# The first pair of token blocks taken block by block over four weight groups, with three attention tiles moved among its products

## The chip, the cores and the metric

The kernel runs on one core of a Trainium2 chip. The metric is device time in microseconds: 1663.98 us is the median of 3 runs (1659.61 to 1665.5). The profiled execution took 1663.56 us; the time from its first instruction to its last, the span, is 1661.8 us.

## The reference

Three layers follow one another on 4608 tokens of width 512.

```python
# 1. attention in chunks of 64 tokens, 8 heads of 64
scores = scale * np.matmul(q_c, k_c.transpose(0, 1, 2, 4, 3))
attn = softmax(scores);  out = np.matmul(attn, v_c)     # -> x, 4608 x 512
# 2. squared ReLU, 512 -> 2048 -> 512
h = np.maximum(x @ w_in, 0.0);  x = h * h @ w_out
# 3. gated unit, 512 -> 1536 -> 512
gate = 1 / (1 + np.exp(-(x @ w_gate)));  out = gate * (x @ w_val) @ w_out
```

The weights arrive as 64-bit floating point numbers and are turned into 32-bit ones on the chip.

## The kernel before

**Number format.** A 32-bit product is made of three products of a reduced format (fp32r). Each operand x is therefore split into a high part, a copy on ACT (L437), and a low part, x minus the high part on DVE (L442).

**Blocks of the product.** A matrix product is done on 2 by 2 blocks with seven products in place of eight. This needs sums of weight blocks (operands "s", "t" and "d", built from POOL's additions at L451) and differences of token blocks. The first pair of token blocks is the exception. It uses the eight plain products, with operand "a" (upper weight blocks) and "l" (lower ones), and no sums.

**A weight tile.** `to_float32` loads 512 KB of a 64-bit weight and turns it into 32 bits: two ACT instructions (L484, L488), three on DVE (L491, L493, L500), one addition on POOL (L507). `split` then makes the high part on ACT and the low part on DVE. So an operand costs DVE four instructions. A group of `w_in` has two such tiles; there are G1 = 8 groups.

**Attention.** A tile has 128 tokens and six tiles are one pair of blocks (BL1 = 384 tokens, three tiles each). Its steps are: load k, q (SP), transpose both on PE and copy on ACT, scores on PE ("S"), a softmax of six DVE instructions (L803 to L812) with one on ACT, a transpose ("T"), load v, the product with v ("X"), and two copies into `raw1[0]` (tiles 0 to 2) or `raw1[1]` (tiles 3 to 5). `attend(0)` does tiles 0 to 5 ahead of all products, `attend(1)` tiles 6 to 11 among the first pair's products, and so on.

**The first pair.** For every group g, `plain_unit` does four results: upper and lower weight block by token block 0, then the same by token block 1. Each result is two calls of `multiply`, six matmuls of 384 columns each.

**What sets the order.** All work is described as jobs, and a planner (`Plan.run`) writes the order out once, before anything runs on the chip. Matmul jobs of the products form one stream that is kept in order; attention's matmuls come in where their written due time ("nominal") is smallest among what is ready. Every other job gets its due time from the job that needs it. An engine takes the ready job that is due first. A job that allocates memory may run only when it is due within its `look` (loads without one: LOOK, others: NEAR). A job that is due further ahead than FAR must leave FLOOR = 8 KB per partition free. `late` in `weight_group` is the look of the sums and of s, t and d. All loads and stores are issued by SP, in the order written.

**After the first pair** come pairs 1 to 5 with seven products (to about 500 us), `w_out` of layer 2 (`long_units`, to about 860 us; its operands are built again from DRAM by `w1out`), the two products of the gate (to about 1390 us), and the last product (`wo`, loaded by `brought`).

Of the kernel before, what the change touches and what calls it, by code (L numbers as in the profile page):

```python
# [51 lines left out]
class Plan:  # L52
# [252 lines left out]
        self.order = order  # L305
        return order

    LOOK, NEAR, HOLD, FAR, FLOOR = 60.0, 15.0, 8.0, 40.0, 8 * 1024

    def stuck(self, t, free, ready, heads, streams, shift):  # L310
        live = {}
# [21 lines left out]
def tile_attention_relu2_glu(  # L333
# [13 lines left out]
    B, H, S, D = q.shape  # L347
# [10 lines left out]
    BL1 = 384  # L358
    TILES = BL1 // P
    scale = 1.0 / float(D) ** 0.5  # L360

    w1i, w1o, wg, wv, w2o = (
        w.bitcast(I32) for w in (moe_w_in, moe_w_out, moe2_w_gate, moe2_w_val, moe2_w_out)
    )
    F1 = moe_w_out.shape[0] // P
    F2 = moe2_w_out.shape[0] // P
    G1, G2 = F1 // 2, F2 // 2
# [530 lines left out]
                self.finish(self, 1, 0, None)  # L898


    def plain_unit(ops, xs, n, per, finish):
        u = Unit(ops, xs, n, per, finish, "")
        for row, col in ((0, 0), (1, 0), (0, 1), (1, 1)):
            ps = psum("C")
            for half in range(2):
                multiply(ps, ops["al"[row]], half, xs[f"B{half + 1}{col + 1}"], n, half == 0, per)
            finish(u, row, col, ps)
# [129 lines left out]
    with tc.manual_schedule():  # L1037

        per1, per, per_h = 0.1735, 0.227, 0.1195
# [5 lines left out]
        w1 = {}  # L1045
# [25 lines left out]
        def attend(s):  # L1071
            for i in range(2 * TILES):
                def nominal(what, i=i):
                    slot = 7 * i + WHEN[what]
                    if s == 0:
                        return -40.0 + 2.0 * i + {"k": 0, "S": 2, "T": 6, "X": 8}[what]
                    if s == 1:
                        return slot * SLOT * 8 / 7
                    return span0 + (s - 2) * span + slot * SLOT
                attention(2 * TILES * s + i, raw1[i // TILES], i // TILES, nominal)  # L1080
# [4 lines left out]
        def finish0(g):  # L1085
            def finish(u, row, col, ps):
                n, f = BL1, g + row * G1
                t = sbuf(n, "e")
                copy(u.words(t), [t], u.words(ps), [ps], n, func=ACTF.Relu)
                if row == col:  # L1090
                    binary("DVE", u.words(t), u.words(ps), u.words(t), ALU.mult, n, [t], [t, ps])
                else:
                    copy(u.words(t), [t], u.words(t), [t], n, func=ACTF.Square, soon=4.0)
                a = col * BL1
                d = gb[f, col] = Buf(name="g")
                dma(lambda: gd[f][:, a:a + n], lambda: at(t), [t], [d], size=P * n * 4, soon=6.0)
            return finish

        attend(0)
        first_xs = {}  # L1100
        for (r, c), x in blocks1(raw1).items():
            name = f"B{r + 1}{c + 1}"
            first_xs[name] = slots1["T1" if name == "B12" else name]
            for op, (src, off) in zip(first_xs[name], x):
                split(op, src, BL1, off=off)
        for g in range(G1):
            w1[g] = weight_group(w1i, g, G1, f"wi{g}", True, look=30.0, late=60.0)
            if g == 1:
                attend(1)
            plain_unit(w1[g], first_xs, BL1, per1, finish0(g))  # L1110
        state = {}

        def unit1(s, g):
# [23 lines left out]
        def brought(back, look):  # L1137
            got = [{} for _ in back]
            for kind in "astd":
                for ops, b in zip(got, back):  # L1140
                    ops[kind] = b[kind](look=look)
            return got


        raws1 = [sbuf(2 * BLK, "wr")], [sbuf(BLK, "wf")], [sbuf(2 * BLK, "ws") for _ in range(2)]
        w1f = [float32_in_dram(rows(w1o, f), f"wf{f}", 130.0, raws1) for f in range(F1)]
# [22 lines left out]
        def y_of(m, a, n):  # L1169
            return [yb[m, b] for b in range(a // BL1, (a + n - 1) // BL1 + 1)]  # L1170

        w1out = [weight_group(None, f, G1, f"wo{f}", True, look=55.0, raws=raws1, by=rows, have=w1f) for f in range(G1)]
        long_units([
            (lambda s=s: Long(w1out, blocks_g(s), BL1, per1, finish_y(s), {"P5": "DVE", "P6": "DVE"})) for s in range(pairs1)
        ])
# [73 lines left out]

        wo = brought(back_o, 80.0)

        def last_blocks(s):
            wide = len(s) == 2
# [68 lines left out]
```

## Time and profile before

| what | value |
|---|---|
| median of 3 runs | 1663.98 us |
| profiled execution | 1663.56 us |
| span of it | 1661.8 us |
| PE busy | 1621.5 us, 98% |
| DVE busy | 1375.4 us, 83% |
| ACT busy | 979.9 us, 59% |
| POOL busy | 822.3 us, 49% |

PE is the matrix engine, PEld its weight loads, DVE the vector engine, ACT the scalar engine, POOL the GpSimd engine, SP the queue that issues transfers. "PEclk" is the granted clock of PE as a share of the full 2.4 GHz; 0.5 would be a stretch wholly at 1.2 GHz. "DMA" is the mean busy share of the 16 transfer engines, as recorded; it can read a little above 1. A row of a timeline gives the start, the duration, the engine, the line, the operation, what is written and read, and in brackets how long the engine was idle before it and what ended that.

### The profile page before, as it was taken

How to read it: one execution, taken by the hardware profiler on the slowest of the kernel's cores; microseconds unless marked ns; L12 is line 12 of the kernel's file. 1: busy time of each engine (PE TensorE's matmuls, PEld its weight loads, DVE VectorE, ACT ScalarE, POOL GpSimd, SP SyncE). 2: the span in 40 equal slices, each digit the busy share in tenths (PEclk: the TensorE clock that was granted, in tenths of full speed). 3: DMA queues.
4: the chain of work that ended last, by engine and by line, in shares of the span. 5: the costliest groups of instructions: out<-in, count | busy, mean ns of one | idle time of the engine just before them, and what ended most of it. 6: DMA issues, size and time to landing. Idle time of an engine off the chain costs nothing. (4 is left out here: it accounts for less than half of the span.)

```text
span 1661.8 us, 30842 instructions
## 1 busy us (share of the span) xinstructions
PE 1621.5 (98%) x10500; PEld 1463.8 (88%) x10500; DVE 1375.4 (83%) x2002; ACT 979.9 (59%) x1968; POOL 822.3 (49%) x636
## 2 busy tenths in 40 slices
PE   7999999999999999999999999999999999999998
PEld 5999999989899999999988888888888888778887
DVE  7998677767789999999999797754777757999995
ACT  6876666665676555565566566544565544454543
POOL 1552103030454443543577677733675646867672
PEclk8999999999999999999999999999999999999999
DMA  9855557666794755855976744496256568665572
GB/s 233 236 137 154 148 149 195 174 185 183 241 303 160 231 191 176 265 184 192 314 264 215 235 169 153 169 342 245 103 202 219 208 244 324 177 183 131 168 176 48
DMA packets 390798, 333.36 MB, mean 201 GB/s; under 512 B 234736, under 2 KB 325616, under 8 KB 390640
## 3 DMA queue, kind: packets, MB, share of 16 engines
q1 hardware_dynamic: 390640, 331.38, 64.4%
q8 instruction: 83, 1.36, 0.3%
q14 instruction: 75, 0.61, 0.1%
HBM read 209.13 MB, written 122.16 MB: 199 GB/s over the span
## 5 line engine op out<-in xcount | busy, mean ns | idle before, releaser
L507 POOL TENSOR_TENSOR wf__3381<-wf__3381,wr__3279 128x512 int32<-128x512 int32 x16 | 21.3, 1331 | 176.5 <-DVE wf__3381 L500 83.6
L507 POOL TENSOR_TENSOR wf__7084<-wf__7084,wr__6460 128x512 int32<-128x512 int32 x18 | 28.4, 1581 | 67.8 <-DMA g__7033<-gd 15.3
L507 POOL TENSOR_TENSOR wf__6751<-wf__6751,wr__6460 128x512 int32<-128x512 int32 x18 | 26.5, 1473 | 65.8 <-DVE wf__6751 L500 37.4
L451 POOL TENSOR_TENSOR raw__514<-raw__674,raw__514 128x384 f32<-128x384 f32 x20 | 23.5, 1195 | 69.2 <-DVE B__762 L442 48.8
L488 ACT ACTIVATE wr__6460<-wr__6460 128x512 int32<-128x512 uint32 x36 | 23.9, 663 | 0.0
L451 POOL TENSOR_TENSOR ws__7370<-wf__6751,wf__7084 128x256 f32<-128x256 f32 x18 | 16.6, 924 | 12.8 <-DVE wx__7053 L442 12.5
L442 DVE TENSOR_TENSOR wx__7053<-ws__7370,wx__7053 128x512 fp32r<-128x512 f32 x18 | 17.7, 984 | 4.1 <-ACT wx__7053 L437 2.2
L442 DVE TENSOR_TENSOR wx__7583<-ws__7370,wx__7583 128x512 fp32r<-128x512 f32 x18 | 18.7, 1041 | 1.9 <-ACT wx__7583 L437 1.9
L442 DVE TENSOR_TENSOR wx__7387<-wf__7084,wx__7387 128x256 fp32r<-128x256 f32 x18 | 17.3, 958 | 2.7 <-ACT wx__7387 L437 2.7
L451 POOL TENSOR_TENSOR ws__7370<-ws__7370,wf__6751 128x256 f32<-128x256 f32 x18 | 15.7, 870 | 1.3
L507 POOL TENSOR_TENSOR w__647<-w__647,wraw__374 128x512 int32<-128x512 int32 x1 | 1.5, 1469 | 29.7 <-ACT w__684 L484 29.7
L493 DVE TENSOR_SCALAR wf__7084<-wf__7084 128x512 int32<-128x512 int32 x18 | 14.2, 790 | 0.6
L484 ACT ACTIVATE wf__6751<-wr__6460 128x512 f32<-128x512 f32 x18 | 12.0, 665 | 4.7 <-POOL ws__7370 L451 4.7
L500 DVE SCALAR_TENSOR_TENSOR wf__7084<-wr__6460,wf__7084 128x512 int32<-128x512 int32 x18 | 14.4, 801 | 0.2
L500 DVE SCALAR_TENSOR_TENSOR wf__6751<-wr__6460,wf__6751 128x512 int32<-128x512 int32 x18 | 14.2, 790 | 0.1
L442 DVE TENSOR_TENSOR B__762<-raw__514,B__762 128x384 fp32r<-128x384 f32 x6 | 3.4, 566 | 13.0 <-ACT B__762 L437 13.0
L484 ACT ACTIVATE wf__7084<-wr__6460 128x512 f32<-128x512 f32 x18 | 11.9, 659 | 2.8 <-DMA wr__6460<-in_moe_w_gate_dram 2.8
L484 ACT ACTIVATE wf__3381<-wr__3279 128x512 f32<-128x512 f32 x16 | 10.6, 665 | 4.3 <-DMA wf<-wf__3381 4.2
L850 ACT ACTIVATE raw__514<-bank 128x256 f32<-128x256 f32 x36 | 12.2, 385 | 1.4 <-PE bank L835 0.5
L451 DVE TENSOR_TENSOR b__12368<-b__12368,bank 128x512 f32<-128x512 f32 x5 | 3.4, 687 | 11.3 <-PE bank L641 11.3
L493 DVE TENSOR_SCALAR wf__6751<-wf__6751 128x512 int32<-128x512 int32 x18 | 12.3, 682 | 0.6
L451 POOL TENSOR_TENSOR sums__2380<-w__1701 128x256 f32<-128x256 f32 x1 | 0.7, 737 | 23.9 <-DVE qT__2187 L751 23.9
(5780 smaller groups left out, 6526.4 us busy)
## 6 DMA issues: line engine op xcount, KB each, us to landing
ad<-wx__7053 SPq DMA_DIRECT2D x27, 512.0 KB, 5.1
ad<-wx__7583 SPq DMA_DIRECT2D x27, 512.0 KB, 4.8
wr__3279<-in_moe_w_out_dram SPq DMA_DIRECT2D x16, 512.0 KB, 4.7
wr__6460<-in_moe_w_gate_dram SPq DMA_DIRECT2D x12, 512.0 KB, 5.5
wr__6460<-in_moe_w_val_dram SPq DMA_DIRECT2D x12, 512.0 KB, 4.6
wr__6460<-in_moe_w_out_dram SPq DMA_DIRECT2D x12, 512.0 KB, 4.1
ad<-wx__7387 SPq DMA_DIRECT2D x18, 256.0 KB, 4.1
wf<-wf__3381 SPq DMA_DIRECT2D x16, 256.0 KB, 4.9
```

Of the source, the lines that this page charges most:

```text
L442: lambda: nc.vector.tensor_tensor(out=lo(), in0=at(src, n, F32, off), in1=hi().bitcast(F32), op=ALU.subtract),
L451: eng, cost(eng, n), lambda: e.tensor_tensor(out=o(), in0=a(), in1=b(), op=op),
L484: nc.scalar.activation(out=at(w), in_=t[:, :, 1].bitcast(F32), func=ACTF.Abs)
L488: nc.scalar.activation(out=low, in_=low.bitcast(U32), func=ACTF.Copy, scale=2.0**-29)
L493: nc.vector.tensor_scalar(out=wi, in0=wi, scalar1=5, scalar2=2, op0=ALU.logical_shift_left, op1=ALU.logical_shift_right,)
L500: nc.vector.scalar_tensor_tensor(out=wi, in0=words()[:, :, 1], scalar=-0x40000000, in1=wi, op0=ALU.bitwise_and, op1=ALU.bitwise_or,)
L507: nc.gpsimd.tensor_tensor(out=wi, in0=wi, in1=words()[:, :, 0], op=ALU.add)
L850: nc.scalar.activation(out=o[:, :, a:a + CH], in_=i, func=ACTF.Copy)
```

## The change

- `plain_unit` takes one token block (`col`) at a time. The order of the products becomes: groups 0 to 3 by token block 0, the same four groups by token block 1, and then groups 4 to 7 as before, block 0 and block 1 of each.
- Tiles 3 to 5 of `attend(0)` get due times among the products: their k and q transposes at -8, -5 and -2 in place of -34, -32 and -30, where the first product is due at 0 and one `multiply` counts 1.04.
- `attend(1)` is described after the third unit; its due times are the same.
- `late` of the `w_in` groups goes from 60 to 30.
- LOOK, NEAR and FAR go from 60, 15, 40 to 90, 20, 55; the look of `w1out` from 55 to 65; that of `wo` from 80 to 60.

```diff
--- before.py
+++ after.py
@@ -305,7 +305,7 @@
         self.order = order
         return order
 
-    LOOK, NEAR, HOLD, FAR, FLOOR = 60.0, 15.0, 8.0, 40.0, 8 * 1024
+    LOOK, NEAR, HOLD, FAR, FLOOR = 90.0, 20.0, 8.0, 55.0, 8 * 1024
 
     def stuck(self, t, free, ready, heads, streams, shift):
         live = {}
@@ -898,9 +898,9 @@
                 self.finish(self, 1, 0, None)
 
 
-    def plain_unit(ops, xs, n, per, finish):
+    def plain_unit(ops, xs, n, per, finish, col):
         u = Unit(ops, xs, n, per, finish, "")
-        for row, col in ((0, 0), (1, 0), (0, 1), (1, 1)):
+        for row in range(2):
             ps = psum("C")
             for half in range(2):
                 multiply(ps, ops["al"[row]], half, xs[f"B{half + 1}{col + 1}"], n, half == 0, per)
@@ -1073,7 +1073,8 @@
                 def nominal(what, i=i):
                     slot = 7 * i + WHEN[what]
                     if s == 0:
-                        return -40.0 + 2.0 * i + {"k": 0, "S": 2, "T": 6, "X": 8}[what]
+                        from_ = -40.0 + 2.0 * i if i < TILES else 3.0 * (i - TILES) - 8.0
+                        return from_ + {"k": 0, "S": 2, "T": 6, "X": 8}[what]
                     if s == 1:
                         return slot * SLOT * 8 / 7
                     return span0 + (s - 2) * span + slot * SLOT
@@ -1103,11 +1104,14 @@
             first_xs[name] = slots1["T1" if name == "B12" else name]
             for op, (src, off) in zip(first_xs[name], x):
                 split(op, src, BL1, off=off)
-        for g in range(G1):
-            w1[g] = weight_group(w1i, g, G1, f"wi{g}", True, look=30.0, late=60.0)
-            if g == 1:
+        AHEAD = 4
+        early = [(g, c) for c in range(2) for g in range(AHEAD)]
+        for i, (g, c) in enumerate(early + [(g, c) for g in range(AHEAD, G1) for c in range(2)]):
+            if c == 0:
+                w1[g] = weight_group(w1i, g, G1, f"wi{g}", True, look=30.0, late=30.0)
+            if i == 3:
                 attend(1)
-            plain_unit(w1[g], first_xs, BL1, per1, finish0(g))
+            plain_unit(w1[g], first_xs, BL1, per1, finish0(g), c)
         state = {}
 
         def unit1(s, g):
@@ -1169,7 +1173,7 @@
         def y_of(m, a, n):
             return [yb[m, b] for b in range(a // BL1, (a + n - 1) // BL1 + 1)]
 
-        w1out = [weight_group(None, f, G1, f"wo{f}", True, look=55.0, raws=raws1, by=rows, have=w1f) for f in range(G1)]
+        w1out = [weight_group(None, f, G1, f"wo{f}", True, look=65.0, raws=raws1, by=rows, have=w1f) for f in range(G1)]
         long_units([
             (lambda s=s: Long(w1out, blocks_g(s), BL1, per1, finish_y(s), {"P5": "DVE", "P6": "DVE"})) for s in range(pairs1)
         ])
@@ -1249,7 +1253,7 @@
 
 
 
-        wo = brought(back_o, 80.0)
+        wo = brought(back_o, 60.0)
 
         def last_blocks(s):
             wide = len(s) == 2
```

## Rows read from the trace of the kernel before

**Rows 1.** Page, part 1: busy time and share of the span by engine

```profile
PE 1621.5 (98%) x10500; PEld 1463.8 (88%) x10500; DVE 1375.4 (83%) x2002; ACT 979.9 (59%) x1968; POOL 822.3 (49%) x636
```

**Rows 2.** Windows of 10 us: busy time by engine, granted clock, DMA

```profile
20.00:30.00 10.00, 7.05 (x180) 5.75 (x176) 9.41 (x22) 7.19 (x17) 0.00 (x0) 0.97 1.06 268
30.00:40.00 10.00, 6.08 (x84) 4.90 (x83) 9.39 (x14) 9.41 (x21) 4.05 (x3) 0.67 1.13 272
40.00:50.00 10.00, 10.00 (x78) 9.43 (x77) 9.86 (x19) 7.75 (x17) 1.61 (x1) 0.84 1.06 267
```

**Rows 3.** Windows, cut at the end of tile 5's softmax, then to 200 us

```profile
0.00:29.15 29.15, 21.10 (x388) 16.97 (x388) 17.70 (x36) 16.73 (x31) 0.70 (x6) 1.00 1.05 215
29.15:60.00 30.85, 26.77 (x273) 24.27 (x274) 29.42 (x49) 26.80 (x57) 12.00 (x10) 0.83 1.10 278
60.00:120.00 60.00, 60.00 (x601) 57.30 (x600) 54.95 (x85) 48.14 (x101) 33.54 (x33) 1.00 0.57 155
120.00:160.00 40.00, 38.89 (x361) 36.49 (x360) 37.09 (x67) 25.42 (x56) 11.49 (x10) 1.00 0.59 157
160.00:200.00 40.00, 40.00 (x422) 37.60 (x421) 25.56 (x51) 24.31 (x56) 5.10 (x6) 1.00 0.62 159
```

**Rows 4.** Timeline of SP's queue: start, duration of the issue, transfer

```profile
9.70 2.01 SPq L415 DMA_DIRECT2D k__317<-in_k_dram  x2
...
21.87 1.79 SPq L415 DMA_DIRECT2D wraw__374<-in_moe_w_in_dram  x1
```

**Rows 5.** Timeline of ACT: first instruction on the first weight

```profile
28.07 0.66 ACT L484 ACTIVATE w__647<-wraw__374 128x512 f32<-128x512 f32 x1 [1.14 <-DMA wraw__374<-in_moe_w_in_dram]
```

**Rows 6.** Timeline of PE: transposes, scores, value product, then the first products

```profile
4.20 1.09 PE L768 MATMUL bank<-ident,k__295 128*128 128x128 f32 x4 [4.20 <-DMA k__295<-in_k_dram]
...
9.29 0.66 PE L768 MATMUL bank<-ident,q__301 128*128 128x128 f32 x4
...
10.63 1.15 PE L785 MATMUL bank<-kT__361,qT__376 64*64 64x64 f32 x32 [0.25 <-ACT qT__376 L422]
...
17.47 0.69 PE L835 MATMUL bank<-aT__480,v__311 64*64 64x64 f32 x32
...
39.50 1.31 PE L641 MATMUL bank<-B__762,wia__734 128*128 128x384 f32 x3
...
44.58 0.68 PE L641 MATMUL bank<-B__762,wil__751 128*128 128x384 f32 x3
45.10 0.68 PE L641 MATMUL bank<-B__767,wil__751 128*128 128x384 f32 x3
```

**Rows 7.** Timeline of DVE: the first softmax, then a weight tile's four instructions

```profile
9.47 0.69 DVE L803 TENSOR_REDUCE mx__372<-bank 128x8 f32<-128x512 f32 x1 [9.47 <-PE bank L785]
...
30.91 0.43 DVE L491 TENSOR_SCALAR w__684<-w__684 128x512 f32<-128x512 f32 x1
31.38 1.40 DVE L493 TENSOR_SCALAR w__684<-w__684 128x512 int32<-128x512 int32 x1
32.81 0.69 DVE L500 SCALAR_TENSOR_TENSOR w__684<-wraw__378,w__684 128x512 int32<-128x512 int32 x1
...
36.20 0.69 DVE L442 TENSOR_TENSOR wil__751<-w__684,wil__751 128x512 fp32r<-128x512 f32 x1
```

**Rows 8.** Timeline of POOL: the first weight's addition

```profile
31.02 1.47 POOL L507 TENSOR_TENSOR w__647<-w__647,wraw__374 128x512 int32<-128x512 int32 x1 [29.72 <-ACT w__684 L484]
```

**Rows 9.** Line L451 alone: results, sums and differences on DVE and POOL

```profile
0.00:60.00 60.00, 1.65 (x3) 3.77 (x4) 0.91 1.07 247
60.00:160.00 100.00, 12.12 (x22) 31.85 (x32) 1.00 0.58 155
```

**Rows 10.** PE in layer 2's second product: a window, and stalls

```profile
520.00:560.00 40.00, 38.01 (x209) 36.86 (x208) 39.05 (x66) 24.66 (x53) 15.01 (x12) 0.96 0.40 124
...
523.49 0.96 PE L961 MATMUL bank<-x__6283,wos__5934 128*128 128x384 f32 x4 [1.40 <-DVE x__6283 L442]
...
856.87 2.26 PE L961 MATMUL bank<-x__9869,wod__6479 128*128 128x384 f32 x6 [3.73 <-ACT x__7925 L437]
```

## The prediction

> **What bounds the kernel now.** I read the busy times by engine first: PE is busy 98% of the span [rows 1], so nothing but PE's own lost time can be won: idle time, and time at half clock. The windows say where it is lost. Up to 60 us PE is busy 21.10 + 26.77 = 47.87 us, 12.1 us idle; from 60 to 120 us it is never idle [rows 3]. In the slices from 30 and from 40 us the granted clock is 0.67 and 0.84 [rows 2]: after work in only 7.05 and then 6.08 of 10 us PE spent part of both slices at 1.2 GHz. Read as a mix of the two levels, that is 6.6 and 3.2 us at half speed, so with the busy share of each slice some (4.0 + 3.2) / 2 = 3.6 us of matmul time is lost. The start thus loses about 16 us. The rest of the run (1661.8 - 1621.5 - 12.1 = 28 us idle, in small stalls and the tail) is not touched directly.
>
> Of the 16 us, 4.2 go before the first k has landed [rows 6], and stay. **About 12 us is the most that the start can give back**, 0.7% of the run.
>
> What does PE wait for up to 39.50 us, where the first product starts [rows 6]? SP issues the first weight at 21.87 us, behind 18 attention loads [rows 4]; it lands at 28.07 [rows 5], 6.2 us later. The transfer engines are full meanwhile (share 1.05 and 1.10 [rows 3]). But DVE is full as well: 9.41, 9.39 and 9.86 of 10 us [rows 2], and 29.42 of the 30.85 us up to 60 us [rows 3]. So two views name two limits, transfers and DVE, and the forecast hangs on which of them the new order meets.
>
> **The change, part by part.** *Tiles 3 to 5 go among the products.* Nine loads (k, q, v of three tiles) move behind the first weights on SP's queue, and the first weight's load moves from 21.87 us to where a fourth tile's k stands now, 9.70 us [rows 4]. It lands at about 16 us. Its conversion takes what it takes now, from 28.07 us to the end of the low part shortly before the same split of the second weight at 36.20 [rows 5, 7], about 7.5 us: ready at 23.5. Token block 0 now waits for tiles 0 to 2 only; I put them at 24 us (before, PE reached the first value product at 17.47 us [rows 6], with four more tiles in the way). The first product then starts at 25 to 26 us in place of 39.50, some 14 us earlier. That is not yet time won, since three tiles' matmuls are still to be done: a tile costs PE three transposes of 0.66, scores of 1.15 and 0.69 for v, in all 3.8 us [rows 6]; three tiles 11.4 us.
>
> *Four groups by block 0, then by block 1.* No matmul is added or taken away. A triple of matmuls follows the one before it by 0.52 us [rows 6], a `multiply` is two of them, 1.04 us, and four groups by one block are 32 triples, 16.7 us. What changes is which operands must be there first. Before, two weight tiles (a and l) feed eight calls, 8.3 us of PE. Now they feed four, 4.2 us, until block 1 has its turn: for the first 16.7 us of products the conversions must come twice as fast.
>
> DVE's bill: six tiles cost it 17.70 us in 36 instructions [rows 3], 2.95 each. From 29.15 to 60 us it did 49 instructions in 29.42 us: two tiles (12 instructions, 5.9 us), three results (1.65 us [rows 9]) and eight token splits of the same 384 columns (4.4); the other 26 instructions, 17.5 us, are 6.5 weight tiles, 2.7 us each. One seen alone is 0.43 + 1.40 + 0.69 + 0.69 = 3.2 [rows 7]; the 1.40 stands beside POOL's addition of 1.47 [rows 8], and with 0.43 in its place the tile would cost 2.2.
>
> Now compare equal PE work. By 60 us PE had done tiles 0 to 6, part of tile 7, and products from 39.50 us on, some 28 triples (20.5 us less two tiles' share, over 0.52). About the same work in the new order is tiles 0 to 6 and all 32 triples of block 0 by four groups. DVE's needs for it: 7 x 2.95 + 4.4 + 4 x 0.55 + 8 x 2.7 = 48.9 us, against 17.70 + 29.42 = 47.1 before: 1.8 us more. Against that stands DVE's idle time, 60 - 47.1 = 12.9 us, of which 9.47 go before the first scores [rows 7] and stay; the earlier weights can fill the other 3.4. So the start lies between 1.8 us lost (nothing filled) and 1.6 won; if conversions met POOL less often (2.2 us each), 8 x 0.5 = 4 more are won. I take 1.5 won, by the DVE rows, which are the nearest. The bounds of this term are 12 won (PE alone limits) and 5 lost (nothing filled, and PE, in short waits, at half clock as long as now).
>
> Here a wait is added: the products are one stream in order, so when group 2's conversion is late, group 0's block 1, ready, stands behind it; only attention's matmuls can pass. From the end of block 0 PE has 16.7 us of products that need no conversion, so DVE catches up.
>
> *late 60 to 30.* The sums on POOL and s, t and d come up to 30 us later. That is 8 x (0.69 + 0.69 + 0.4) = 14 us of DVE (the 0.69 is a 512-column split [rows 7], d has half) and part of POOL's 31.85 us at L451 [rows 9]. They cost nothing where DVE has room: 2.9 us from 120 to 160 and 14.4 us from 160 to 200 [rows 3]. If that cover fails, pair 1 waits for them. I take zero, bounds 1 won (PE's 1.1 us idle from 120 to 160 [rows 3]) and 7 lost (rival C).
>
> The Trainium skill, "SBUF — State Buffer", section "SBUF: two separate sides", says that VectorE and GpSimd share a port pair that one instruction holds to its end while the other fully blocks. The row of 1.40 us beside the 1.47 us addition agrees. By that rule each POOL sum that leaves the start gives DVE up to its own length back, at most the 3.77 us of four sums before 60 us [rows 9]; the start would then win 5 in place of 1.5, still less than half a per cent.
>
> *Limits.* Each load that allocates has a look of its own, so LOOK changes nothing. NEAR lets splits and copies take memory 5 us earlier, FAR lets work 40 to 55 us ahead use the last 8 KB: no price in the trace; zero, bounds 4 us either way, one stall like that of 3.73 us at 856 us [rows 10]. `w1out` may load 10 us earlier: at 523 us PE waits 1.40 us for a split on DVE, and from 520 to 560 us it is idle 2.0 us at a granted clock of 0.96 [rows 10], 3.2 us at half speed, 1.6 lost: 3.6 in all. I take half, 2 won, bounds 0 and 3.6. `wo` from 80 to 60: PE's idle time does not show that these loads are late or early; zero, bounds as for NEAR.
>
> **Sum.** 1663.56 - 1.5 - 2 = 1660 us. The profiled execution (span 1661.8 and 1.8 around it) is 0.4 below the median of 1663.98, which I let stand.
>
> **Rivals.** *B, PE alone limits the start.* For it: PE gets products 14 us earlier. Against it: DVE's 94 to 99% from 20 us on [rows 2]. By 25.5 us PE has then done three tiles and half of tile 3, about 13.5 us, and 2 us more for the cold first matmuls (1.09 against 0.66 [rows 6]): 10 idle. If it is full from there, 16 - 10 = 6 are won, and up to 12 if more of tiles 3 to 5 comes before; I take 8. With the 2 of `w1out`: 1653.5, from 1649 to 1656.
>
> *C, slower: the work put off is owed at the border of pairs 0 and 1.* Place: 125 to 145 us, in the window in which DVE is 37.09 of 40 us busy [rows 3]. If half of the 14 us of s, t and d falls there, into 2.9 us of room, PE waits 4 us. After the stall of 3.73 us the next six matmuls took 2.26 us [rows 10] against 1.04 for two triples: 2 more for the clock. With 2.5 lost at the start: 1663.6 + 8.5 = 1672. It decides once more than 2.9 us of DVE work is put off into that window.
>
> The Trainium skill, "TensorE: Matmul & The Clock Gate", section "Part 1: The HAM clock gate (the "warmup" mystery)", says that half rate is the default and only activity lifts it, which speaks against a stream of short waits; the 0.67 after a thin slice agrees, and the 5 lost above hold it.
>
> *D, the longer limits.* Memory given out earlier holds up blocks of tokens at one or two of the later borders, 3.73 and 2 us each like the stall at 856 us [rows 10]: 1670. Against it: the loads there have their own looks, unchanged but for two.
>
> **Chances.** Forecast 0.55 (own range 1655 to 1667), B 0.29, C 0.11, D 0.05. About 0.5%, 8.3 us, is what a measurement of this kernel can tell from no change. B mostly lies beyond it (0.24), the forecast's low edge adds 0.06: faster 0.30. C and most of D: slower 0.14. The rest, 0.56, is the same. The range from 1650 to 1671 leaves out half of C and the ends.
>
> **What would show it.** The first product at 25 to 26 us (forecast and B alike); DVE over 9.4 of 10 us from 20 to 60 us with PE idle between weight tiles (forecast), or PE over 9.5 of 10 from 26 us on (B); PE's idle time up to 60 us at 9 to 13 us (forecast), 7 or less (B); a wait of PE over 2 us for an s, t or T operand between 125 and 180 us (C); the stall near 523 us gone. A first product after 30 us, or a time outside 1650 to 1671, would make it wrong.

## The result, and the profile after

The changed kernel takes 1673.08 us (median of 5 runs, 1670.61 to 1675.06) against 1662.74 us for the kernel before (5 runs, 1659.61 to 1665.5). The ratio is 1.0062, interval 1.0051 to 1.0074: **slower**, 10 us and 0.6%, outside the forecast range of 1650 to 1671. The profiled execution took 1673.64 us.

The page of the kernel after, busy time by engine, answers to [rows 1]:

```profile
PE 1624.1 (97%) x10500; PEld 1463.9 (88%) x10500; DVE 1364.1 (82%) x2002; ACT 980.9 (59%) x1968; POOL 811.2 (49%) x636
```

PE's busy time grew by 2.6 us and the span by 10.1 (1671.9 - 1661.8), so 7.5 us are new idle time. The other engines worked about as long or less.

Where the time went is read best at an equal point of the work. Layer 2's second product (L961) begins after 4704 recorded matmuls in both kernels. Windows of the two kernels up to that point, and for 56.75 us behind it; the columns are the stretch, its length, then busy us and count of PE, PEld, DVE, ACT and POOL, the granted clock, DMA share and GB/s. First the kernel before:

```profile
0.00:503.25 503.25, 482.38 (x4704) 453.40 (x4705) 397.44 (x706) 340.33 (x733) 144.76 (x138) 0.99 0.72 196
503.25:560.00 56.75, 54.76 (x305) 53.61 (x305) 55.38 (x90) 34.51 (x76) 25.20 (x20) 0.97 0.52 168
```

The same two stretches of the kernel after:

```profile
0.00:509.44 509.44, 483.84 (x4704) 454.51 (x4705) 386.86 (x707) 340.39 (x735) 142.54 (x136) 0.98 0.71 195
509.44:566.19 56.75, 52.36 (x281) 49.55 (x281) 54.24 (x86) 33.86 (x71) 25.85 (x22) 0.97 0.44 147
```

By the first L961 the new kernel is 6.2 us late: 4.7 us more idle time (25.60 against 20.87) and 1.5 us more for the same matmuls, part of them at half clock. In the next 56.75 us it does 281 matmuls in place of 305; 24 at 0.174 us (a triple of 0.52) are 4.2 us. The sum, 10.4, is the loss. The other 1100 us are even.

The first 6.2 us, by stretch. Windows of the kernel after, the first three for [rows 2], the others for [rows 3 and 10] and the end of the pairs:

```profile
20.00:30.00 10.00, 7.30 (x150) 5.93 (x148) 8.16 (x13) 8.38 (x20) 2.90 (x3) 0.90 1.17 277
30.00:40.00 10.00, 8.75 (x157) 7.68 (x160) 9.83 (x22) 9.85 (x21) 1.74 (x2) 1.00 0.94 243
40.00:50.00 10.00, 8.08 (x96) 7.23 (x89) 9.79 (x18) 8.14 (x18) 3.18 (x3) 1.00 0.92 221
...
0.00:60.00 60.00, 46.70 (x665) 40.25 (x666) 46.96 (x87) 42.94 (x87) 11.19 (x14) 0.94 1.05 236
60.00:120.00 60.00, 60.00 (x596) 56.88 (x596) 45.72 (x78) 45.36 (x92) 25.21 (x24) 1.00 0.63 169
120.00:160.00 40.00, 36.31 (x337) 34.55 (x336) 30.45 (x57) 23.89 (x54) 11.50 (x12) 0.96 0.49 134
160.00:200.00 40.00, 40.00 (x425) 37.62 (x424) 29.42 (x57) 26.84 (x61) 10.87 (x13) 1.00 0.65 165
...
520.00:560.00 40.00, 35.61 (x185) 32.80 (x184) 38.79 (x62) 21.18 (x44) 17.42 (x15) 0.96 0.29 93
```

- *Start, 0 to 60 us:* 13.3 us idle (12.1 before), but less time at 1.2 GHz. Read as a mix of the two levels, a clock of 0.94 over 60 us is 7.2 us at half speed; at a busy share of 0.78, half of it is lost, 2.8 us. Before, 0.83 over the last 30.85 us [rows 3] gave 10.5 us, 4.6 lost. So the start is even within a microsecond, 16.1 us lost against 16.7; by 120 us PE has done 1261 recorded matmuls, against 1262.
- *Border of pairs 0 and 1, 120 to 160 us:* 3.7 us idle (1.1 before) at a clock of 0.96 (1.00 before), 1.4 us by the same reckoning: 4 us lost.
- *End of the pairs, 440 us to the first L961:* the rest, some 2 us, in stalls of 1.81 us and less at 450 us and a slice behind them at a clock of 0.83.

**The start.** The weight's issue on SP, its first ACT instruction, what ACT, DVE and POOL did before the first product, and that product, from the timelines of the kernel after (start, duration, engine, line, operation; in brackets idle time and what ended it). They answer to [rows 4, 5 and 6].

```profile
9.68 1.32 SPq L415 DMA_DIRECT2D wraw__317<-in_moe_w_in_dram  x1
...
16.82 0.66 ACT L484 ACTIVATE w__477<-wraw__317 128x512 f32<-128x512 f32 x1
...
21.35 1.34 POOL L507 TENSOR_TENSOR w__477<-w__477,wraw__317 128x512 int32<-128x512 int32 x1 [20.04 <-DVE w__477 L500]
...
21.57 1.40 DVE L493 TENSOR_SCALAR w__528<-w__528 128x512 int32<-128x512 int32 x1
...
24.46 0.68 ACT L850 ACTIVATE raw__491<-bank 128x256 f32<-128x256 f32 x2
...
24.62 1.36 DVE L442 TENSOR_TENSOR wia__566<-w__477,wia__566 128x512 fp32r<-128x512 f32 x1 [0.92 <-ACT wia__566 L437]
26.70 0.43 DVE L491 TENSOR_SCALAR w__577<-w__577 128x512 f32<-128x512 f32 x1 [0.71 <-ACT w__577 L484]
...
28.56 0.60 ACT L437 ACTIVATE B__629<-raw__491 128x384 fp32r<-128x384 f32 x1
...
31.65 0.69 DVE L812 TENSOR_TENSOR a__623<-a__623,mx__371 128x512 f32<-128x512 f32 x1
32.26 0.55 DVE L442 TENSOR_TENSOR B__629<-raw__491,B__629 128x384 fp32r<-128x384 f32 x1
...
34.48 0.79 PE L641 MATMUL bank<-B__629,wia__566 128*128 128x384 f32 x3
```

The weight was there as early as forecast, and its low part was done at 26.0 us. The last piece of token block 0 was copied from 24.46 us on. But ACT then did copies of tiles 3 and 4 and parts of two weight tiles, and made the high part (B__629, L437) only at 28.56 us. DVE did the third weight tile, the softmax of tile 3 and the first steps of tile 4's without a gap, and made the low part at 32.26 us. Loads do not set the first product; the orders on ACT and DVE do.

**The border.** SP's queue in the kernel after:

```profile
121.51 8.18 SPq L415 DMA_DIRECT2D ql__1826<-in_q_dram  x16
...
131.74 0.40 SPq L415 DMA_DIRECT2D gd<-e__790  x1
132.31 0.38 SPq L415 DMA_DIRECT2D k__1981<-in_k_dram  x1
```

and PE there:

```profile
130.83 1.15 PE L785 MATMUL bank<-kT__1950,qT__1781 64*64 64x64 f32 x32 [1.36 <-ACT kT__1950 L422]
...
136.63 0.66 PE L768 MATMUL bank<-ident,k__1981 128*128 128x128 f32 x4 [2.33 <-DMA k__1981<-in_k_dram]
...
138.38 1.16 PE L641 MATMUL bank<-B__629,wia__756 128*128 128x384 f32 x3
```

One q load, issued as 16 transfers, holds SP for 8.18 us. Five stores follow, and only then the k that PE stands for; behind the stall a triple takes 1.16 us in place of 0.69. DVE had 9.5 us to spare in the window, so this is not the lack of DVE time that rival C named. Nor is it the q load alone. The kernel before has two such loads here, from 112.65 us (8.52 us) and from 126.81 us, and loses only 1.1 us in the window: PE waits there for no load that stands behind them. The second one, from SP's timeline of the kernel before:

```profile
126.81 8.88 SPq L415 DMA_DIRECT2D ql__1939<-in_q_dram  x16
```

**The entry of layer 2's second product.** PE in the kernel after, for the stall at 523 us of [rows 10], which is gone; the last row answers to its stall at 856.87 us, which is not:

```profile
530.12 0.97 PE L961 MATMUL bank<-x__6490,wos__6235 128*128 128x384 f32 x4 [0.40 <-DVE x__6490 L442]
...
535.51 0.44 PE L961 MATMUL bank<-x__6490,wos__6557 128*128 128x384 f32 x1 [0.73 <-DVE wos__6557 L442]
536.78 1.20 PE L961 MATMUL bank<-x__6490,wos__6557 128*128 128x384 f32 x4 [0.83 <-DVE x__6490 L442]
...
558.45 1.14 PE L961 MATMUL bank<-x__6800,wot__6860 128*128 128x384 f32 x5 [1.14 <-DVE wot__6860 L442]
...
867.58 1.52 PE L961 MATMUL bank<-x__8014,wod__6293 128*128 128x384 f32 x6 [3.63 <-DVE b__2909 L451]
```

One wait of 1.40 us became a row of small ones, each for a low part on DVE, which was busy 38.79 of 40 us. The stall at 867 us has about the size of the old one, but another releaser.

### The profile page after: what moved, and what is told of

It reads as the page before. It is cut to its first block, busy times and chain, and to the rows that moved or that the text cites. A ratio compares the mean times of both kernels' runs of the same rounds, so it can differ in the third digit from the quotient of the medians.

```text
span 1671.9 us, 30839 instructions
## 1 busy us (share of the span) xinstructions
PE 1624.1 (97%) x10500; PEld 1463.9 (88%) x10500; DVE 1364.1 (82%) x2002; ACT 980.9 (59%) x1968; POOL 811.2 (49%) x636
## 4 chain that ended last, share of the span: by engine, by line
PE 82%; DVE 8%; issue 3%; DMA 3%; ACT 2%; POOL 2%; SPq 1%; DVEq 0%; ACTq 0%; POOLq 0%
PE bank L641 48%; PE bank L961 29%; PE bank L785 2%; PE bank L835 1%; PE bank L819 1%; PE bank L768 1%; SPq L415 1%; DVE x__14566 L442 0%; DMA k__333<-in_k_dram 0%; DMA wr__6475<-in_moe_w_val_dram 0%; DMA yd<-c__7381 0%; POOL wf__6611 L507 0%; DMA k__299<-in_k_dram 0%; DMA gd<-c__2147 0%; DVE x__14547 L442 0%
## 5 line engine op out<-in xcount | busy, mean ns | idle before, releaser
L451 POOL TENSOR_TENSOR raw__491<-raw__774,raw__491 128x384 f32<-128x384 f32 x20 | 24.9, 1267 | 58.8 <-DVE B__629 L442 38.7
L491 DVE TENSOR_SCALAR wf__7093<-wf__7093 128x512 f32<-128x512 f32 x18 | 13.4, 744 | 8.4 <-ACT wf__7093 L484 8.4
L451 DVE TENSOR_TENSOR b__10757<-b__10757,bank 128x512 f32<-128x512 f32 x9 | 6.2, 684 | 14.7 <-PE bank L641 14.7
L451 POOL TENSOR_TENSOR ws__7383<-wf__6611,wf__7093 128x256 f32<-128x256 f32 x18 | 16.4, 912 | 0.1
L491 DVE TENSOR_SCALAR wf__6611<-wf__6611 128x512 f32<-128x512 f32 x18 | 12.6, 697 | 4.7 <-ACT wf__6611 L484 4.7
L451 POOL TENSOR_TENSOR ws__7383<-ws__7383,wf__6611 128x256 f32<-128x256 f32 x18 | 15.0, 835 | 1.1
L484 ACT ACTIVATE wf__7093<-wr__6475 128x512 f32<-128x512 f32 x18 | 11.9, 660 | 4.6 <-DMA wr__6475<-in_moe_w_val_dram 4.0
L451 DVE TENSOR_TENSOR b__11976<-b__11976,bank 128x512 f32<-128x512 f32 x5 | 3.4, 688 | 13.2 <-PE bank L641 9.5
L500 DVE SCALAR_TENSOR_TENSOR wf__6611<-wr__6475,wf__6611 128x512 int32<-128x512 int32 x18 | 13.3, 739 | 0.2
L451 POOL TENSOR_TENSOR g__7004<-g__6141,g__7004 128x384 f32<-128x384 f32 x2 | 6.2, 3118 | 14.7 <-PE bank L961 11.0
L484 ACT ACTIVATE wf__3407<-wr__3301 128x512 f32<-128x512 f32 x16 | 10.7, 666 | 4.4 <-DMA wf<-wf__3407 4.4
```

Source lines behind the costliest of these rows:

```text
L451: eng, cost(eng, n), lambda: e.tensor_tensor(out=o(), in0=a(), in1=b(), op=op),
L484: nc.scalar.activation(out=at(w), in_=t[:, :, 1].bitcast(F32), func=ACTF.Abs)
L491: nc.vector.tensor_scalar_max(at(w), at(w), TINY)
L500: nc.vector.scalar_tensor_tensor(out=wi, in0=words()[:, :, 1], scalar=-0x40000000, in1=wi, op0=ALU.bitwise_and, op1=ALU.bitwise_or,)
```

## The experiments

The first theory after the comparison was that work put off by the shorter `late` is owed at the border and at the entry; its rivals were that the new start or the limits do the harm, and, from the first experiments on, that any edit gives another order whose stalls fall anew, as if drawn by lot ("a draw" below).

"Idle" is PE's idle time, the length less PE's busy time in a window, in us. Ratios are to the kernel before, timed beside each.

| kernel | median us | ratio, interval | idle 0-60 | 120-160 | 500-560 |
|---|---|---|---|---|---|
| before | 1662.7 | 1 | 12.1 | 1.1 | 2.0 |
| after | 1673.1 | 1.0062, 1.0051 to 1.0074 | 13.3 | 3.7 | 5.6 |
| 1 before + new start + late 30 | 1689.3 | 1.0161, 1.0144 to 1.0178 | 16.0 | 5.7 | 8.6 |
| 2 before + limits | 1658.0 | 0.9972, 0.9962 to 0.9982 | 10.2 | 1.5 | 3.3 |
| 3 before + late 30 | 1671.6 | 1.0055, 1.0041 to 1.0069 | 13.2 | 5.6 | 6.8 |
| 4 before + w1out 65 | 1656.4 | 0.9964, 0.9951 to 0.9977 | 12.7 | 1.1 | 2.1 |
| 5 after, late 60 | 1670.1 | 1.0046, 1.0033 to 1.0059 | 13.0 | 1.6 | 7.8 |
| 6 after, old start, late 60 | 1662.8 | 1.0007, 0.9996 to 1.0017 | 10.6 | 1.7 | 3.2 |
| 7 before + block order | 1665.5 | 1.0020, 1.0009 to 1.0030 | 11.9 | 1.9 | 3.7 |
| 8 before, late 58 | 1662.5 | 1.0001, 0.9992 to 1.0009 | 12.5 | 1.5 | 2.9 |
| 9 before, late 45 | 1674.5 | 1.0068, 1.0053 to 1.0084 | 11.7 | 2.1 | 7.5 |
| 10 before + tiles' due times | 1677.8 | 1.0091, 1.0078 to 1.0104 | 15.3 | 4.1 | 3.2 |
| 11 after, late 32 | 1668.8 | 1.0040, 1.0028 to 1.0052 | 13.4 | 2.5 | 5.5 |
| 12 before, late 90 | 1671.1 | 1.0050, 1.0037 to 1.0062 | 13.8 | 1.7 | 10.9 |
| 13 before, margin 1.6 | 1735.7 | 1.0426, 1.0409 to 1.0442 | | | |
| 14 after, margin 1.6 | 1814.4 | 1.0903, 1.0887 to 1.0919 | | | |
| 15 before, issue 0.46 | 1664.8 | 1.0005, 0.9996 to 1.0015 | 12.2 | 1.5 | 2.1 |
| 16 after, issue 0.46 | 1662.9 | 0.9999, 0.9989 to 1.0009 | 14.1 | 1.6 | 2.9 |
| 17 before, debt 0.44 | 1666.9 | 1.0031, 1.0021 to 1.0040 | 12.4 | 1.6 | 5.9 |
| 18 after, debt 0.44 | 1677.6 | 1.0105, 1.0084 to 1.0125 | 12.2 | 4.6 | 3.7 |

The three stretches are not the whole run. From 160 to 440 us experiments 1 and 18 have 13.6 and 10.1 us idle, the kernel before 4.8, and the others but 13 and 14 1.4 to 6.2. The idle times are each of one execution, and the table leaves out time at 1.2 GHz.

**1. The start and the shorter `late`, without limits and looks.** The kernel before with the new `plain_unit`, loop and tile times, and

```diff
-            w1[g] = weight_group(w1i, g, G1, f"wi{g}", True, look=30.0, late=60.0)
+                w1[g] = weight_group(w1i, g, G1, f"wi{g}", True, look=30.0, late=30.0)
```

> The kernel before with the new start alone: products by token block over four groups, tiles 3 to 5 among them, late at 30; LOOK, NEAR, FAR and the looks of w1out and wo as before. Theory of places (each loss belongs to the edit that touches its place): the stalls of PE near 130 to 140 us stay (about 3.8 us of idle time and slow clock), the loss between 440 and 560 us (about 6 us) is gone: about 1666.5 us, 4 over before. Rival, the theory of rewriting (any edit rewrites the whole order, and stalls fall anew by chance all over the run): the first 120 us as in the changed kernel, and from there a loss or gain of up to 6 us anywhere, not tied to these two places.

1689.3 us, the slowest of the parts: 16.0 us idle at the start, 5.7 at the border, 13.6 from 160 to 440 us, 8.6 from 500 to 560. The first product stands at 37.64 us, not at 34.48.

**2. The limits alone.**

```diff
-    LOOK, NEAR, HOLD, FAR, FLOOR = 60.0, 15.0, 8.0, 40.0, 8 * 1024
+    LOOK, NEAR, HOLD, FAR, FLOOR = 90.0, 20.0, 8.0, 55.0, 8 * 1024
```

> The kernel before with LOOK, NEAR and FAR at 90, 20 and 55, and nothing else. Theory of places: the start and the border of pairs 0 and 1 as before; part of the loss at 440 to 560 us, where operands for w_out are loaded more than 40 us ahead and FAR applies: 3 us slower, about 1666. Theory of rewriting: anywhere from 1658 to 1670, with stalls at other borders than in the changed kernel.

4 us faster. The first product of this kernel, from PE's timeline:

```profile
34.47 0.67 PE L641 MATMUL bank<-B__741,wia__734 128*128 128x384 f32 x1
```

The first product comes at 34.47 us with the *old* order of tiles: the 5 us that the change seemed to win there are had by the limits alone, and PE's idle time up to 60 us is 10.2. Taken over the run, the limits by themselves cost nothing, against rival D, though 2.4 us of new idle time stand between 60 and 120 us.

**3. `late` alone.** The edit of experiment 1's diff, on the kernel before.

> The kernel before with late at 30 in place of 60, and nothing else: the sums and s, t, d of w_in come later. If the work put off is what stalls the border of pairs 0 and 1 (rival C of the prediction): 3 to 4 us of new PE idle time between 125 and 145 us, 1666 us. If the border stalls for its k loads, which this edit does not touch: no new idle time there, 1663 us give or take 2. Theory of rewriting: 1658 to 1670.

9.6 us slower, by itself as much as the whole change. PE's timeline at the border, and then the window:

```profile
136.03 0.73 PE L819 MATMUL bank<-ident,a__1980 128*128 128x128 f32 x4 [3.05 <-DVE a__1980 L812]
```

```profile
120.00:160.00 40.00, 34.37 (x326) 32.31 (x325) 35.79 (x62) 24.30 (x53) 15.99 (x16) 0.96 0.52 133
```

Here PE does wait for DVE, but for a softmax, and not for want of DVE time. DVE was busy 35.79 us in the window, less than the 37.09 before [rows 3], and stood idle before it took up this softmax, until PE had its scores:

```profile
130.41 0.69 DVE L803 TENSOR_REDUCE mx__1971<-bank 128x8 f32<-128x512 f32 x1 [0.72 <-PE bank L785]
```

The place is the same as in the kernel after, the releaser is not. That the work put off causes this wait is not shown.

**4. The look of `w1out` alone.**

```diff
-        w1out = [weight_group(None, f, G1, f"wo{f}", True, look=55.0, raws=raws1, by=rows, have=w1f) for f in range(G1)]
+        w1out = [weight_group(None, f, G1, f"wo{f}", True, look=65.0, raws=raws1, by=rows, have=w1f) for f in range(G1)]
```

> The kernel before with the look of w1out at 65 in place of 55, and nothing else. The order up to about 430 us is the same by construction, so its PE idle time up to there must be as before. By the prediction: 2 us won near 523 us, 1661. Theory of places now: the loss at 440 to 560 us comes from this edit, 4 to 6 us slower, 1667 to 1669.

6 us faster, the best kernel of all; it beats both. Its windows for [rows 10] and the 300 us behind them:

```profile
520.00:560.00 40.00, 38.87 (x220) 37.71 (x219) 39.44 (x66) 23.25 (x48) 13.52 (x12) 1.00 0.39 128
...
600.00:900.00 300.00, 297.96 (x1660) 289.77 (x1658) 290.73 (x422) 186.18 (x368) 166.99 (x124) 1.00 0.68 228
```

From 520 to 560 us it does 220 matmuls in place of 209, at a clock of 1.00, not 0.96: 11 at 0.174 are 1.9 us, the size that the forecast took. The rest is elsewhere: from 600 to 900 us PE is idle 2.0 us against 6.6, since the stall of 3.73 us at 856 us is gone. Nothing in the edit aims at that stall. Part of the gain is no matter of order: the edit leaves the order alone up to about 430 us, and the traces agree up to 120 us, where PE, DVE and SP have the same instructions in the same order. Yet in this execution the two slices of [rows 2] that had a clock of 0.67 and 0.84 read

```profile
30.00:40.00 10.00, 5.38 (x85) 4.07 (x83) 9.83 (x15) 8.94 (x20) 4.18 (x3) 0.86 1.08 268
40.00:50.00 10.00, 10.00 (x87) 9.40 (x85) 9.86 (x20) 8.51 (x19) 1.63 (x1) 0.97 1.14 277
```

By the prediction's reckoning that is 1.0 us lost to the clock in place of 3.6, so a clock term moves by some 2.5 us from one execution to the next. The 6 us of the medians stand beyond that.

**5. and 6. The kernel after with `late` 60, and that with the old start too.**

```diff
-                w1[g] = weight_group(w1i, g, G1, f"wi{g}", True, look=30.0, late=30.0)
+                w1[g] = weight_group(w1i, g, G1, f"wi{g}", True, look=30.0, late=60.0)
```

> The changed kernel with late back at 60, all else as changed. If late at 30 is what stalls the border of pairs 0 and 1 (late alone cost 9 us): the PE idle time near 125 to 150 us goes, and 5 to 9 us come back: 1664 to 1668 us, no slower than before within 0.3%. If the new start itself costs (tiles 3 to 5 and block order): 1672 or more.

> The kernel before with LOOK, NEAR, FAR, the looks of w1out and wo as changed, and the old start with late at 60. The limits alone won 4 us and w1out alone 5.6. Theory of places (gains belong to their edits and add up): 1652 to 1655. Theory of rewriting (each is one draw of an order): 1657 to 1663, no better than each alone.

With the same limits, looks and `late`, the old start takes 1662.8 us and the new one 1670.1: the new start costs 7 us. Idle time up to 60 us is 2.4 more; at 500 to 560 us, a stretch that holds no work of the start, it is 4.6 more. The border is nearly whole in both. Putting `late` back gives 3 of the 10 us back, and the intervals of experiment 5 and the kernel after overlap. The parts that gain alone (4 and 6 us) gain nothing together with the look of `wo` at 60. `wo` alone was not run; from 900 to 1400 us, experiment 6 has 7.1 us idle, experiments 2 and 4 have 6.5 and 5.3 without that edit.

**7. and 10. The start in its two halves,** first the new `plain_unit` and its loop as in the change, then the due times of tiles 3 to 5 (the edit below), each alone on the kernel before.

```diff
-                        return -40.0 + 2.0 * i + {"k": 0, "S": 2, "T": 6, "X": 8}[what]
+                        from_ = -40.0 + 2.0 * i if i < TILES else 3.0 * (i - TILES) - 8.0
+                        return from_ + {"k": 0, "S": 2, "T": 6, "X": 8}[what]
```

> The kernel before with the first pair's products by token block over four groups, tiles 3 to 5 and late as before, and no other edit. If the block order alone asks too much of DVE (twice the conversions in the first 16.7 us of products): PE idle between 40 and 60 us, 3 to 6 us lost by 60 us, 1666 to 1669 at the end. If conversions keep up because all six tiles come first: no loss by 60 us, 1662 give or take 3.

> The kernel before with the due times of tiles 3 to 5 as changed, and no other edit. Theory: moving them behind the first weights gains nothing by itself, since DVE and ACT, not the loads, set the first product; the first product comes 2 to 5 us earlier, PE lost time by 60 us the same within 1.5 us, 1662 give or take 3. If the loads had been the limit: first product at 26 us, 5 us won by 60 us, 1657.

The order by blocks costs 3.4 us, the tiles' times 15. In experiment 10 the first product comes at 40.30 us, later than before: moving tiles 3 to 5 behind the weights does not by itself bring the products forward. Neither half gains, though in the old order of results block 1, and with it tiles 3 to 5, is due four calls, 4.2 us, after the first product.

**8., 9. and 12. Other values of `late`** on the kernel before: 58, 45 and 90 in place of 60. Theory: what counts is how much work is put off, so the time grows as `late` falls. Rival: any change of the number gives another order, with stalls of its own.

```diff
-            w1[g] = weight_group(w1i, g, G1, f"wi{g}", True, look=30.0, late=60.0)
+            w1[g] = weight_group(w1i, g, G1, f"wi{g}", True, look=30.0, late=58.0)
```

> The kernel before with late at 58 in place of 60: an edit too small to move work by itself, but the planner writes a new order. Theory of places: 1662 within 1.5 us. Theory of rewriting: the time moves by 2 to 6 us either way, which would be the scatter against which every single edit's gain or loss has to be read.

> The kernel before with late at 45, half of the step. Late at 30 cost 9.6 us, late at 58 nothing. Theory of debt (work put off falls due where DVE is full, so the cost grows with the delay): 2 to 6 us slower, 1664 to 1668, with new PE idle time between 125 and 155 us. Theory of draws (each order is a new draw): no order between the steps, 1656 to 1670, and where it loses is not the border of pairs 0 and 1.

> The kernel before with late at 90, the other way. Theory of debt: the sums come as soon as their weights do, DVE and POOL have them behind them at the border of pairs 0 and 1: the 2 us lost there go or stay, 1660 to 1663. If early sums instead take DVE from the first weights: 2 to 4 us lost between 40 and 120 us, 1665.

Against 60, the values 30, 45, 58 and 90 cost 10, 12, 0 and 9 us. The longest is as bad as the shortest, so the time does not follow the work put off. But 58 moved nothing, against the rival: not every edit is a new draw of several us. The place of the loss follows it in part: at 45 and 90 the border is nearly whole (2.1 and 1.7 us idle), and the entry of layer 2 takes the loss. PE there with 90:

```profile
522.26 0.69 PE L961 MATMUL bank<-x__6481,woa__6167 128*128 128x384 f32 x1 [7.88 <-ACT woa__6167 L437]
525.94 1.97 PE L961 MATMUL bank<-x__6481,woa__6167 128*128 128x384 f32 x5 [2.99 <-DVE woa__6167 L442]
```

**11. The kernel after with `late` 32** in place of 30, the same edit.

> The changed kernel with late at 32 in place of 30, an edit too small to move work, but a new order. Theory of places: 1673 within 1.5 us, with the stalls at the border of pairs 0 and 1 and in the first unit of layer 2's second product as in the changed kernel. Theory of draws: the 10 us of the changed kernel are partly chance, 1664 to 1676, with stalls of other sizes at these two places.

4 us faster than with 30, from two units of a due time.

**13. to 18. Both kernels with a cost of the planner nudged,** in three pairs: the margin of a transfer, the cost of an issue on SP, and the share in which POOL's use of the port counts against DVE. None of these numbers changes an instruction; they change what the planner believes.

```diff
-    DMA_LATENCY, MARGIN = 2.5, 1.5
+    DMA_LATENCY, MARGIN = 2.5, 1.6
...
-        return job("SP", 0.45 * n, go, reads, writes, size=size, soon=soon, look=look)
+        return job("SP", 0.46 * n, go, reads, writes, size=size, soon=soon, look=look)
...
-                    port["debt"] += 0.45 * min(cost, max(0.0, port["DVE"] - t))
+                    port["debt"] += 0.44 * min(cost, max(0.0, port["DVE"] - t))
```

> The kernel before with the planner's margin for a transfer at 1.6 in place of 1.5: no part of the change, a new order. Theory of the change (the 10 us belong to the edits): 1662 within 2 us here, and 1673 within 2 us for the changed kernel with the same nudge. Theory of draws (each order is a draw with a scatter of several us, and before was an ordinary or a lucky one): 1658 to 1675 here, and the two kernels nudged alike differ by anything from -8 to +12.

> The changed kernel with the planner's margin for a transfer at 1.6 in place of 1.5. Theory of the change: 1673 within 2 us, 10 over its partner. Theory of draws: 1660 to 1680.

> The kernel before with the planner's cost of a transfer's issue at 0.46 in place of 0.45 us: no part of the change, a new order. Theory of the change: 1662 within 2 us. Theory of draws: 1658 to 1675, the loss mostly in the first 40 us of layer 2's second product, where the orders so far lost between 2 and 14 us.

> The changed kernel with the planner's cost of a transfer's issue at 0.46 in place of 0.45 us. Theory of the change: 1673 within 2 us, 10 over its partner, 3 to 4 us of it at the border of pairs 0 and 1. Theory of draws: 1660 to 1680.

> The kernel before with the planner's factor for time that DVE owes POOL at 0.44 in place of 0.45: no part of the change, a new order, the third such pair. Theory of the change: 1662 within 2 us. Theory of draws: 1658 to 1675.

> The changed kernel with the same factor at 0.44 in place of 0.45. Theory of the change: 1673 within 2 us, 10 over its partner. Theory of draws: 1660 to 1680, and the mean of the three differences of pairs is below 5 us.

After less before is +79, -1.9 and +10.7 us in the three pairs, a mean of 29 us and not below 5. The margin breaks both kernels, beyond everything expected, mostly by one wait of PE each; first experiment 14, then experiment 13:

```profile
345.52 0.69 PE L641 MATMUL bank<-T__981,wis__2850 128*128 128x384 f32 x1 [122.87 <-ACT wis__2850 L437]
```

```profile
478.32 1.33 PE L641 MATMUL bank<-T__1994,wit__2587 128*128 128x384 f32 x3 [42.94 <-ACT c__5378 L422]
```

In experiment 14 the wait is for an operand s of `w_in`, an operand whose look `late` sets. What fills both waits are conversions of `w_out` to 32 bits, which go through one buffer (`wr`, `wf`) one after another, some 8.6 us each: load, convert, store. SP in experiment 14:

```profile
222.25 0.33 SPq L415 DMA_DIRECT2D wr__1329<-in_moe_w_out_dram  x1
222.63 0.42 SPq L415 DMA_DIRECT2D wf<-wf__2618  x1
231.00 0.33 SPq L415 DMA_DIRECT2D wr__1329<-in_moe_w_out_dram  x1
```

Fourteen of them in a row stand in the orders of ACT, DVE and POOL ahead of what PE waits for, and five in experiment 13. In the kernels before and after, the stores of all sixteen are spread from 252 to 497 us. So the margin pair shows one failure of the written order, of work without haste ahead of work that is due, and says little of the scatter of the others. Why the planner placed it so was not traced.

In experiment 18 the stall of the kernel after comes again in its place, with the k load on SP behind a q load of 16 transfers and five stores:

```profile
136.62 1.12 PE L768 MATMUL bank<-ident,k__2002 128*128 128x128 f32 x4 [4.61 <-DMA k__2002<-in_k_dram]
```

In experiment 16 it does not, nor the loss at the entry: 1.6 and 2.9 us idle, and the kernel is as fast as before. So the change can cost nothing; its slowness hangs on the order written. In experiment 18 the border is not the whole loss either: 10.1 us are idle from 160 to 440 us.

## Why the prediction was wrong

The step that failed is the sum. Each of its terms is priced only at the wait at which an edit aims, and no term stands for what the new order does elsewhere. Added one after another, limits and looks (experiment 6) measured about 1 us lost, the start (experiment 5) 7 lost and the shorter `late` (the change) 3 lost; forecast were 2 won, 1.5 won and zero. Alone, the same edits measure otherwise, so this split is one of several.

- *The start, 1.5 us won, bounds 12 won and 5 lost:* about right in its own stretch, even. The reason given, that DVE is full, is not shown. DVE was full from 30 to 60 us (9.83, 9.79 and 9.82 of 10 us) but not from 20 (8.16), and the earlier weights filled none of its idle time (13.0 us by 60 us, 12.9 before). Of PE's 9.1 us idle up to 60 us after the first k, the profile puts 6.0 to copies on ACT, 1.9 to a load of k and 1.0 to DVE. So the size held in part by luck. What the term left out is the rest of the run: with equal settings the new start costs 7 us (experiments 5 and 6), 4.6 of it idle from 500 to 560 us. PE's idle time of 13.3 us lies just past the 9 to 13 named. Rival B, with PE at 9.5 of 10 from 26 us on, is false: 8.75 and 8.08.
- *The first product at 25 to 26 us:* wrong, 34.48. The steps to the weight held (issue 9.68, ACT at 16.82, low part at 26.0 against 23.5 forecast). The step that failed is "Token block 0 now waits for tiles 0 to 2 only": its splits also waited for ACT and DVE, behind the third weight tile and tiles 3 and 4. It cost the forecast nothing, since the sum was made from DVE's bill and not from this moment.
- *The sums of POOL leave the start:* they did; L451 has no POOL instruction up to 60 us, four before [rows 9]. The 3.5 us more that this would give by the rule of the Trainium skill ("SBUF — State Buffer", section "SBUF: two separate sides") did not show: a conversion still took 1.40 us (at 21.57 us) beside an addition of POOL of 1.34 us that belongs to the weight itself.
- *"late 60 to 30 ... I take zero":* wrong. Alone it costs 9.6 us (experiment 3), beyond its bound of 7; in the change about 3 (experiment 5). In the kernel after, 4 us are lost at the border, 2.6 in idle time and 1.4 by the clock. Rival C had the place, and 6 us as the price there; its cause, no room on DVE, is shown in neither kernel. In experiment 3 a softmax is late with DVE less busy than before, and in the kernel after the k load is late on SP's queue with DVE a quarter idle. The wait over 2 us that was named for C is there, for k and not for s, t or T. Leaving out the margin pair, idle time at the border was 1.6 to 5.7 us in the six kernels with `late` 30 or 32 (mean 4.0); in the twelve others it was 1.1 to 2.1, but for 4.1 in experiment 10. So a shorter `late` goes with losses at the border; it does not decide them.
- *"`w1out` ... I take half, 2 won" and limits "zero":* wrong. Alone they won 6 and 4 us, the first beyond its bound of 3.6; together with `wo` they won nothing (experiment 6). The 4.2 us lost at the entry stand in the very place where 2 were to be won. The stretch from 500 to 560 us, where DVE has next to no room (39.05 of 40 us [rows 10]), had 2.9 to 10.9 us idle in the kernels that edit only the start or `late` (experiments 1, 3, 7 to 10 and 12), against 2.0: edits of the start or of `late` go with stalls there, far from where they aim.
- *Size of the draw.* Without the margin pair, the kernels that differ from the kernel before by one number of the ordering (experiments 3, 4, 8, 9, 12, 15 and 17) lie between 1656.4 and 1674.5 us. The smallest edits alone (8, 15 and 17) lie at 1662.5 to 1666.9; the change with `late` 32 or a nudge (11, 16 and 18), and as it is, at 1662.9 to 1677.6. The means of these two kinds, the kernel before counted in, are 1664.2 and 1670.6. The bounds of 4 us for "limits" were made from single stalls, and no term for the draw stood in the sum or the range.

**What stays open:** how much of the 10 us belongs to the change and how much to the order drawn. Added as above, with equal settings the new start costs 7 us and the shorter `late` 3 more (experiments 6, 5, after), but a nudged issue cost takes all of it back (experiment 16). The changed kernels lean slower, by 6 us in the means of four kernels each; with a spread of 15 us among the changed ones, four do not give a size. What makes the entry of layer 2 early or late was not settled either.

## What to carry to other kernels

When a planner writes a static order for engines that are 80 to 98% busy, an edit of due times or looks can give a new order to the end of the run: price it with the scatter of neighbouring settings (here 4 us about the kernel before, 15 about the changed one, 18 over all settings of one number), not by the one stall at which it aims, and do not add the gains of single edits. Before crediting or blaming such an edit, run both kernels with one planner cost nudged; keep the edits that win alone, here the look of `w1out` at 65 (1656.4 us) or the limits (1658.0 us), and look for the best draw. Where one nudge costs 70 us or more, read the order for work without haste that holds all engines in a row. Work that is put off needs room on every queue at its new time, the issuing queue too, not only on the engine that does it.

## What the runs showed of the hardware

- One q load of 16 transfers held SP's queue for 8.18 us in the kernel after (8.15 in experiment 18), 0.51 us each, and a k load behind it cost PE 2.33 and 4.61 us, though the transfer engines were busy only 0.49 of the window from 120 to 160 us in the kernel after. An issuing queue can be the limit while its transfers have room. The load alone does not do it: the kernel before has loads of 8.52 and 8.88 us here without such a wait.
- The same order met different clocks in two executions: 0.67 and 0.84 of full speed from 30 to 50 us in the kernel before, 0.86 and 0.97 in experiment 4.
- DVE's 2002 instructions took 1364.1 us in place of 1375.4, and POOL's 636 took 811.2 in place of 822.3, the same instructions in another order, each in one execution. That fewer of them met may be the reason; no run tested it. PE gained nothing from it.
